# Half-row matmuls in sections of three feature groups, and eight PSUM banks dealt out anew, in a scan and gated-MLP kernel

## The chip, the cores and the metric

The kernel runs on one core of one Trainium2 chip. The metric is the device time of one execution, in microseconds (us), as the median of several runs. TensorE (PE) does the matmuls and writes to PSUM, which has eight banks of 2 KB in each of 128 partitions; ScalarE (ACT) and VectorE (DVE) read PSUM and do the element-wise work; GpSimd (POOL) does small constants; SyncE (SP) issues the DMAs. Each engine works through its own list of instructions, and semaphores tie the lists together.

## The reference

The input `x` has 2048 tokens of 448 features. It is normalised per token, and the result feeds two branches:

```python
def _A_ref(x, ...):                       # a diagonal complex recurrence over the tokens
    Lam_bar = jnp.exp(dt * Lam)
    Bu = jnp.einsum("bld,pd->blp", x + 0j, B_bar)
    for t in range(L):
        h = Lam_bar[None, :] * h + Bu[:, t, :]
        hs.append(h)
    return 2.0 * jnp.einsum("blp,dp->bld", hseq, Cmat).real + x * Dskip

def _B_ref(x, w_gate, w_up, w_down):      # a gated MLP, 448 -> 1792 -> 448
    h = _sigmoid(x @ w_gate) * (x @ w_up)
    return h @ w_down

xn = _layernorm(x)
return x + _A_ref(xn, ...) * _silu(_B_ref(xn, ...))
```

All data is bf16; the recurrence has 448 complex states.

## The kernel before

**Chunks.** The tokens are worked in four chunks of 512 (`NCH`, `TC`), and each chunk in four token tiles of 128. Features lie on the partitions: `xnT[c]` holds the normalised chunk, transposed. The 448 features are three full tiles of 128 rows and one half tile of 64.

**Gate and up.** The 1792 hidden features are 14 groups of 128 (`ft`). For a group, the gate matmuls add up in one PSUM bank and the up matmuls in another: three "wholes" each, over 128 rows (`gu_wholes`, L618), and one "half" each, over the last 64 rows (`gu_halves`, L611). The gate's half uses rows 0 to 63 of the array and the up's half rows 64 to 127, so the two run as a pair, side by side. In `emit_gu`, an even group runs its wholes and then its halves, an odd group its halves and then its wholes; so the halves of two groups stand together, and TensorE goes from 128-row to 64-row work and back once for two groups. Such a stretch of halves is called a section here. `gu_out` then has ScalarE take the sigmoid of the gate (`sig`, L635) and copy the up (`ub`, L639), and VectorE multiply the two (`hF`, L644); the multiplication of one group is put into the list when the next group's `gu_out` is written.

**Recurrence.** For a chunk and a tile `pt` of the states, `bu_halves` (L469) and `emit_bu` (L480) form the input of the recurrence, real and imaginary in one bank each (the last tile, of 64 states, has both in one bank). Its halves stand in the section of an odd group. ScalarE copies the banks (`bus`, L489, L549), and VectorE's pieces follow: `p0` to `p2`, two scans, `p3` to `p5` for the full tiles (L495 to L530), `q0` to `q7` for the last one (L555 to L591). For the last tile the two halves of the partitions are exchanged by a pair of DMAs, once before `q1` (`bsw`) and once before `q5` (`wsw`, L460, L461). The result is the state tile `h`.

**Down, y and the end.** `emit_down` (L660) multiplies a token tile of the finished chunk's `hF` by `w_down` into a bank `d`; ScalarE reads it twice (`sigd`, `zb`), and VectorE forms the gate `g_t`. `emit_y` (L682 to L688) sums the states' outputs into a bank `y`, and `emit_fin` (L695, L697) multiplies by the gate, adds `x` and stores. Down products of a chunk stand between the groups of the next chunk, y behind them.

**Order.** `keep_order` fixes every engine's list as the program writes it. VectorE's pieces wait in the list `pieces`; each call of `fill(pe, own)` moves a clock on by one and a budget `room` by what TensorE's work beside it is taken to last, and puts pieces into the list while there is room and the wait that a piece names (in ticks since the one before) is over. Extra work (statistics of the next chunk's x, the constants, `emit_c` with `c_tmp`, the transposes `tc_re` and `tc_im`, loads) is hung on a group with `at(c, ft, ...)` and written behind that group.

**Banks.** The PSUM pool has the tags `g` and `u` with two banks each and `acc` with four; `acc` serves `bu`, `d` and `y`, and in the opening the transposes `tp_x` and the gate and up of the third and fourth group. Banks of a tag are used in turn, and a tile waits until the one that held its bank before has been read.

**Opening.** The first four groups of chunk 0 run in two column halves of 256, as soon as the first two token tiles are normalised.

Of the kernel before, what the change touches and what calls it, by code (L numbers as in the profile page):

```python
# [10 lines left out]
FP32 = mybir.dt.float32  # L11
BF16 = mybir.dt.bfloat16
# [51 lines left out]
def kernel(  # L64
# [122 lines left out]
    warm_ps = ps.tile([P, P], FP32, name="warm_ps", tag="u")  # L187
# [74 lines left out]
    def ln_out(j, tp, copy):  # L262
        copy(out=xnT[0][:, :, j * P:(j + 1) * P], in_=tp[:])  # L263
# [28 lines left out]
    def emit_vecs():  # L292
        tp = ps.tile([P, KT, 4], BF16, name="tp_v", tag="g")
        turn_twice(tp, rows, 4)
        vec = w.tile([P, KT, 4], FP32, name="vec")
        dve.tensor_copy(out=vec[:], in_=tp[:])
        dt_b = w.tile([P, KT], BF16, name="dt_b")
        act.activation(dt_b[:], vec[:, :, 0], ACT.Exp)
        K.update(dt=dt_b, lim=vec[:, :, 1], lre=vec[:, :, 2], dsk=vec[:, :, 3])
# [154 lines left out]
    def bank(spare, tag, name):  # L454
        if spare:
            return ps.tile([P, TC], FP32, name=name, tag="acc", bufs=4)
        return ps.tile([P, TC], FP32, name=name, tag=tag)
# [16 lines left out]
    def emit_bu(c, pt, pst):  # L474
# [71 lines left out]
        else:  # L546
# [47 lines left out]
            for cost, f, wait in ((0.42, q0, 1), (0.42, q1, 1), (0.42, q2, 0), (1.27, q3, 0), (0.42, q4, 0),  # L594
                                  (0.42, q5, 2), (0.0, q6, 0), (0.42, q7, 0)):
                later(cost, f, wait)
# [23 lines left out]

    def emit_gu(c, ft, beside_halves=None):
        gt, ut = bank(False, "g", "g_ps"), bank(False, "u", "u_ps")
        if ft % 2 == 0:
            gu_wholes(c, ft, gt, ut, True, up_first=(c == 0 and ft == 4))
            gu_halves(c, ft, gt, ut, False)
        else:
            gu_halves(c, ft, gt, ut, True)
            if beside_halves is not None:
                beside_halves()
            gu_wholes(c, ft, gt, ut, False)  # L630
        gu_out(c, ft, gt, fp.tile([P, TC], BF16, name="ub"), ut)
# [25 lines left out]
    def emit_down(c, j):  # L657
        d = ps.tile([P, D], FP32, name="d_ps", tag="acc", bufs=4)
# [18 lines left out]
    def emit_y(c, j, d0=0, d1=D):  # L677
        y = ps.tile([P, D], FP32, name="y_ps", tag="acc", bufs=4)
# [69 lines left out]
    tps = [ps.tile([P, KT + 1, P], BF16, name="tp_x", tag="acc", bufs=4) for _ in range(TPC)]  # L748

    def norm0(j):  # L750
        ln_norm(0, j)
        ln_turn(0, j)
# [7 lines left out]
    act.activation(K["r"][:], K["arg"][:], ACT.Exp)  # L760
    ln_root(0, 2, 2, True)
    ln_out(0, tps[0], dve.tensor_copy)
# [6 lines left out]
    gus = [(bank(ft > 1, "g", "g_ps"), bank(ft > 1, "u", "u_ps")) for ft in range(4)]  # L769
# [8 lines left out]
    ln_out(3, tps[3], dve.tensor_copy)  # L778
    for ft in range(4):
        gu_halves(0, ft, *gus[ft], ft == 3, 0, HC)  # L780
    gu_wholes(0, 3, *gus[3], False, 0, HC)
    gu_wholes(0, 3, *gus[3], True, HC, TC)
    for ft in (3, 0, 1, 2):
        gu_halves(0, ft, *gus[ft], ft < 3, HC, TC)
    for ft in range(3):
        gu_wholes(0, ft, *gus[ft], False, HC, TC)
# [45 lines left out]
    bu_q, out_q, bu_pst = [], [], []  # L832
    room[0] = -2.0
    for c in range(NCH):
        bu_q.extend((c, pt) for pt in range(KT))
        for ft in range(4 if c == 0 else 0, FT):
            bu = None
            if ft % 2 == 1 and (4 if c == 0 else 0) < ft < FT - 1 and bu_q and unread[0] < 2:
                bu = bu_q.pop(0)
                emit_gu(c, ft, lambda: bu_pst.append(bu_halves(*bu)))  # L840
            else:
                emit_gu(c, ft)
            emit_gate()
            for cost, f in beside.pop((c, ft), ()):
                room[0] -= cost
                f()
            fill(1.62 if c < NCH - 1 or ft < 9 else 2.2, 0.42)
            if ft % 2 == 0:
                continue
            if bu is not None:  # L850
                emit_bu(*bu, bu_pst.pop())
                popped[0] = clock[0]
                fill(1.5, 0.0)
            if c == 0:
                continue
            if ft < 8:
                emit_down(c - 1, ft // 2)
                fill(2.66, 0.39)
                if ft == 7:
                    out_q.extend((c - 1, j) for j in range(TPC))  # L860
            if c == NCH - 1 and ft == FT - 1:
                emit_mul()
            for _ in range(2 if ft == 11 else 1):
                if not (out_q and ft >= 8 and all((out_q[0][0], pt) in hs for pt in range(KT))):
                    break
                emit_y(*out_q[0])
                emit_fin(*out_q.pop(0))
                fill(1.53, 1.01)
    flush()

# [6 lines left out]
    def outs(j, d0=0, d1=D):  # L877
        emit_y(c, j, d0, d1)
        emit_fin(c, j, d0, d1)

    for j in range(2):
        down(j)
        outs(j)
    down(2)
    down(3)
    outs(2)
# [33 lines left out]
```

## Time and profile before

| | |
|---|---|
| three runs | 193.56, 193.94 and 194.0 us; median 193.94 |
| the profiled execution | 193.69 us, of which the span from first to last instruction is 191.9 us |
| TensorE busy | 186.2 us (97%), 1080 matmuls, granted clock 1.00 |
| VectorE busy | 156.4 us (81%) |
| ScalarE busy | 111.1 us (58%) |
| GpSimd busy | 49.3 us (26%) |
| DMA | 14.87 MB in all, mean 77 GB/s |

In the lines of a timeline the columns are: start in us from the span's start, length in us, engine, line of the program, operation, output <- inputs, shapes, how many instructions are merged, and in brackets the idle time before them with what ended it. A line of the waits reads: who waited, for whom, us in total, how often, the longest. Matmuls overlap, so the time from start to start, not the length, is what one costs. L numbers are lines of the kernel before; in the changed kernel the same statements stand some ten lines higher (L623 and L627 for `sig` and `ub`, L632 for `hF`, L648 for d, L670 and L672 for y, L683 for `sg`).

### The profile page before, as it was taken

The numbers are of one execution on the slowest core, as the hardware profiler recorded it, in microseconds if no ns is written. First come the engines' busy times: TensorE is split into PE (matmuls) and PEld (weight loads), VectorE is DVE, ScalarE is ACT, GpSimd is POOL, SyncE is SP. The second block draws the span as 40 slices with busy tenths as digits, with TensorE's granted clock in tenths as the row PEclk, the third lists the DMA queues.
The fourth block names the chain that finished last, engine by engine and source line by source line (L and its number), as shares of the span: only waits on it lengthen the run. The fifth ranks groups of instructions, "written<-read, shape, count | busy, mean of one in ns | idle before, by whom it ended". The sixth has DMA issues, their size and how long they took to land.

```text
span 191.9 us, 3117 instructions
## 1 busy us (share of the span) xinstructions
PE 186.2 (97%) x1080; PEld 89.1 (46%) x1080; DVE 156.4 (81%) x315; ACT 111.1 (58%) x213; POOL 49.3 (26%) x98
## 2 busy tenths in 40 slices
PE   7899999999999999999999999999999999999992
PEld 6765433344444445444444444444444444545552
DVE  3889799937999699999985979997649999995224
ACT  4997776557499775454556586245746744242240
POOL 3885399940043025030321020304020000000000
PEclk9999999999999999999999999999999999999999
DMA  5998993994410123601001000530010010021101
GB/s 145 310 301 160 254 112 70 321 286 105 90 31 0 36 87 88 97 26 29 0 5 27 0 0 24 108 89 16 0 27 3 0 27 0 26 65 38 44 6 48
DMA packets 27592, 14.87 MB, mean 77 GB/s; under 512 B 16308, under 2 KB 27576, under 8 KB 27576
## 3 DMA queue, kind: packets, MB, share of 16 engines
q1 hardware_dynamic: 27568, 14.67, 32.7%
q8 instruction: 8, 0.13, 0.3%
q14 instruction: 8, 0.07, 0.2%
q10 hardware_dynamic: 8, 0.00, 0.0%
HBM read 8.38 MB, written 1.84 MB: 53 GB/s over the span
## 4 chain that ended last, share of the span: by engine, by line
PE 91%; DMA 4%; DVE 2%; SPq 1%; issue 0%
PE d_ps L660 22%; PE g_ps L618 20%; PE u_ps L618 18%; PE bu L480 9%; PE y_ps L682 9%; PE g_ps L611 7%; DMA b_re<-in_A_B_re_dram 2%; PE bu L469 2%; PE y_ps L688 2%; PE y_ps L684 1%; DMA x<-in_A_x_dram 1%; DVE sg L695 1%; DVE frac L398 1%; DVE xn L243 0%; DVE o_t L697 0%
## 5 line engine op out<-in xcount | busy, mean ns | idle before, releaser
L635 ACT ACTIVATE sig<-g_ps 128x512 bf16<-128x512 f32 x56 | 33.1, 597 | 36.8 <-PE u_ps L611 32.4
L618 PE MATMUL g_ps<-xnT,wg 128*128 128x512 bf16 (+1 forms) x180 | 46.4, 366 | 0.2 <-DVE xnT L263 0.2
L618 PE MATMUL u_ps<-xnT,wu 128*128 128x512 bf16 (+1 forms) x180 | 45.9, 365 | 0.0
L660 PE MATMUL d_ps<-wd,hF 128*128 128x448 bf16 x224 | 44.8, 352 | 0.0
L639 ACT CAST ub<-u_ps 128x512 bf16<-128x512 f32 x52 | 30.3, 583 | 2.1 <-PE u_ps L618 0.4
L660 PEld LDWEIGHTS <-hF 128*128 128x128 bf16 x224 | 21.7, 98 | 20.5
L663 ACT ACTIVATE sigd<-d_ps 128x448 bf16<-128x448 f32 x16 | 8.7, 543 | 32.4 <-PE d_ps L660 30.4
L618 PEld LDWEIGHTS <-wu 128*128 128x128 bf16 x180 | 17.6, 98 | 18.5
L644 DVE TENSOR_TENSOR hF<-sig,ub 128x512 bf16<-128x512 bf16 x56 | 23.5, 423 | 2.2 <-ACT ub L639 2.1
L618 PEld LDWEIGHTS <-wg 128*128 128x128 bf16 x180 | 14.7, 98 | 22.0 <-issue 12.0
L508 DVE TENSOR_TENSOR_SCAN wv<-r_col,st,ta 128x512 bf16<-128x512 f32 x18 | 22.7, 1273 | 0.2
L682 PE MATMUL y_ps<-ct,h 128*128 128x448 bf16 (+1 forms) x102 | 21.0, 342 | 0.0
L480 PE MATMUL bu<-xnT,bT 128*128 128x512 bf16 x84 | 20.7, 379 | 0.0
L515 POOL TENSOR_TENSOR tq<-wv,smT 128x2 f32<-128x2 bf16 x9 | 5.3, 585 | 56.2 <-DVE wv L508 56.2
L611 PE MATMUL u_ps<-xnT,wt 64*128 64x512 bf16 (+1 forms) x60 | 17.0, 367 | 0.1
L611 PE MATMUL g_ps<-xnT,wt 64*128 64x512 bf16 (+1 forms) x60 | 17.0, 367 | 0.0
L669 DVE TENSOR_TENSOR g_t<-zb,sigd 128x448 bf16<-128x448 bf16 x16 | 6.2, 390 | 11.9 <-ACT zb L665 11.9
L489 ACT CAST bus<-bu 128x512 bf16<-128x512 f32 x24 | 13.6, 592 | 0.5
L207 DVE BATCH_NORM_STATS2 stats<-x 128x6 f32<-128x448 bf16 x14 | 8.6, 617 | 6.2 <-DMA x<-in_A_x_dram 6.2
L682 PEld LDWEIGHTS <-h 128*128 128x128 bf16 x102 | 9.6, 98 | 8.2
L480 PEld LDWEIGHTS <-bT 128*128 128x128 bf16 x84 | 8.2, 98 | 9.9
L695 DVE TENSOR_TENSOR sg<-y_ps,g_t 128x448 bf16<-128x448 f32 (+1 forms) x17 | 10.0, 588 | 0.9 <-PE y_ps L688 0.5
(135 smaller groups left out, 225.3 us busy)
## 6 DMA issues: line engine op xcount, KB each, us to landing
out_dram<-o_t SPq DMA_DIRECT2D x15, 112.0 KB, 1.8
wd<-in_B_w_down_dram SPq DMA_DIRECT2D x1, 1568.0 KB, 7.7
x<-in_A_x_dram SPq DMA_DIRECT2D x3, 448.0 KB, 3.6
wg<-in_B_w_gate_dram SPq DMA_DIRECT2D x2, 384.0 KB, 5.2
wu<-in_B_w_up_dram SPq DMA_DIRECT2D x2, 384.0 KB
wg<-in_B_w_gate_dram SPq DMA_DIRECT2D x1, 576.0 KB, 4.4
wu<-in_B_w_up_dram SPq DMA_DIRECT2D x1, 576.0 KB, 6.5
bsw<-bus SPq DMA_DIRECT2D x8, 64.0 KB, 2.0
```

Of the source, the lines that this page charges most:

```text
L480: pe.matmul(pst[:], lhsT=bT[:, kt, lo:hi], rhs=xnT[c][:, kt, :], start=False, stop=(kt == 2))
L489: act.copy(out=bus[:, cc, :], in_=pst[cc][:])
L508: dve.tensor_tensor_scan(out=T["wv"][:, cc, :], data0=rb, data1=T["ta"][:, cc, :], initial=(0.0 if c == 0 else st[pt][:, cc, :]), op0=mul, ...
L611: pe.matmul(t[:, n0:n1], lhsT=wt[p0:p0 + 64, f0:f1], rhs=xnT[c][p0:p0 + 64, KT if c == 0 and p0 else 3, n0:n1], start=first, stop=not first)
L618: pe.matmul(t[:, n0:n1], lhsT=wm[:, kt, f0:f1], rhs=xnT[c][:, kt, n0:n1], start=(first and kt == 0), stop=(not first and kt == 2))
L635: act.activation(sig[:], gt[:], ACT.Sigmoid)
L639: act.copy(out=ub[:], in_=ut[:])
L644: dve.tensor_tensor(out=h[:], in0=sig[:], in1=ub[:], op=ALU.mult)
L660: pe.matmul(d[:], lhsT=hF[c, ft][:, j * P:(j + 1) * P], rhs=wd[:, ft, :], start=(ft == 0), stop=(ft == FT - 1))
L663: act.activation(sigd[:], d[:], ACT.Sigmoid)
L682: pe.matmul(y[:, d0:d1], lhsT=hs[c, pt][:, cc, sl], rhs=ct[:, 2 * pt + cc, d0:d1], start=(pt == 0 and cc == 0), stop=False)
L695: dve.tensor_tensor(out=sg[:, d0:d1], in0=ys[c, j][:, d0:d1], in1=gs[c, j][:, d0:d1], op=ALU.mult)
```

## The change

- Banks: `g` and `u` get three banks each, `acc` two.
- Groups are worked in sections of three, at a chunk's end of two: chunk 0 in groups 4-6, 7-9, 10-11, 12-13; the others in 0-2, 3-5, 6-8, 9-11, 12-13. In a section, all groups but the last run their wholes, then all halves stand together, with those of a bu, then the last group runs its wholes.
- Extra work that hangs on a group is written behind that group's wholes for all but the last of a section (before its `gu_out`), and behind the `gu_out` of the last.
- Per chunk there are five sections (four in chunk 0) and so five chances for a bu; a bu is taken while fewer than three are unread (before: two). Chunk 0 takes four. Chunks 1 and 2 take theirs in their sections 0, 1, 3 and 4, chunk 3 in 0 to 3.
- Down products stand one each behind sections 0 and 1 and two behind section 2; y in pairs behind sections 3 and 4. In the end, d(3,1) stands ahead of y(3,0), and y uses the banks of `u`.
- The waits of `q1` and `q5`, in ticks, go from 1 and 2 to 2 and 3.
- In the opening, the fourth group starts with its wholes, and its halves of the first columns stand in the second section; the transposes' tiles are made when they are needed.

```diff
-    warm_ps = ps.tile([P, P], FP32, name="warm_ps", tag="u")
+    warm_ps = ps.tile([P, P], FP32, name="warm_ps", tag="u", bufs=3)
...
     def bank(spare, tag, name):
         if spare:
-            return ps.tile([P, TC], FP32, name=name, tag="acc", bufs=4)
-        return ps.tile([P, TC], FP32, name=name, tag=tag)
+            return ps.tile([P, TC], FP32, name=name, tag="acc", bufs=2)
+        return ps.tile([P, TC], FP32, name=name, tag=tag, bufs=3)
...
-            for cost, f, wait in ((0.42, q0, 1), (0.42, q1, 1), (0.42, q2, 0), (1.27, q3, 0), (0.42, q4, 0),
-                                  (0.42, q5, 2), (0.0, q6, 0), (0.42, q7, 0)):
+            for cost, f, wait in ((0.42, q0, 1), (0.42, q1, 2), (0.42, q2, 0), (1.27, q3, 0), (0.42, q4, 0),
+                                  (0.42, q5, 3), (0.0, q6, 0), (0.42, q7, 0)):
...
-    def emit_gu(c, ft, beside_halves=None):
...
-    def emit_y(c, j, d0=0, d1=D):
-        y = ps.tile([P, D], FP32, name="y_ps", tag="acc", bufs=4)
+    def emit_y(c, j, d0=0, d1=D, tag="acc", bufs=2):
+        y = ps.tile([P, D], FP32, name="y_ps", tag=tag, bufs=bufs)
...
-    tps = [ps.tile([P, KT + 1, P], BF16, name="tp_x", tag="acc", bufs=4) for _ in range(TPC)]
+    tps = []
     def norm0(j):
+        tps.append(ps.tile([P, KT + 1, P], BF16, name="tp_x", tag="acc", bufs=2))
...
-    gus = [(bank(ft > 1, "g", "g_ps"), bank(ft > 1, "u", "u_ps")) for ft in range(4)]
+    gus = [(bank(False, "g", "g_ps"), bank(False, "u", "u_ps")) for _ in range(3)]
...
+    gus.append((bank(True, "g", "g_ps"), bank(True, "u", "u_ps")))
+    for ft in range(3):
+        gu_halves(0, ft, *gus[ft], False, 0, HC)
+    gu_wholes(0, 3, *gus[3], True, 0, HC)
+    gu_halves(0, 3, *gus[3], False, 0, HC)
     for ft in range(4):
-        gu_halves(0, ft, *gus[ft], ft == 3, 0, HC)
-    gu_wholes(0, 3, *gus[3], False, 0, HC)
-    gu_wholes(0, 3, *gus[3], True, HC, TC)
-    for ft in (3, 0, 1, 2):
-        gu_halves(0, ft, *gus[ft], ft < 3, HC, TC)
-    for ft in range(3):
+        gu_halves(0, ft, *gus[ft], True, HC, TC)
+    for ft in range(4):
         gu_wholes(0, ft, *gus[ft], False, HC, TC)
...
+    def rest(c, ft):
+        emit_gate()
+        for cost, f in beside.pop((c, ft), ()):
+            room[0] -= cost
+            f()
+
+    def section(c, units, bu):
+        gb, more = {}, 0.6 if c == NCH - 1 and units[0] >= 9 else 0.0
+        pre, post = units[:-1], units[-1]
+        for ft in pre:
+            gb[ft] = (bank(False, "g", "g_ps"), bank(False, "u", "u_ps"))
+            gu_wholes(c, ft, *gb[ft], True, up_first=(c == 0 and ft == 4))
+            rest(c, ft)
+            fill(1.3 + more, 0.0)
+        for ft in pre:
+            gu_halves(c, ft, *gb[ft], False)
+        gb[post] = (bank(False, "g", "g_ps"), bank(False, "u", "u_ps"))
+        gu_halves(c, post, *gb[post], True)
+        pst = None if bu is None else bu_halves(*bu)
+
+        def out(ft):
+            gu_out(c, ft, gb[ft][0], fp.tile([P, TC], BF16, name="ub"), gb[ft][1])
+
+        out(pre[0])
+        fill(0.2 + 0.22 * len(units), 0.42)
+        if bu is not None:
+            emit_bu(*bu, pst)
+            popped[0] = clock[0]
+            fill(1.5, 0.0)
+        if len(pre) > 1:
+            out(pre[1])
+            room[0] -= 0.42
+        gu_wholes(c, post, *gb[post], False)
+        out(post)
+        rest(c, post)
+        fill(1.3 + more, 0.42)
...
+        cuts = (4, 7, 10, 12, 14) if c == 0 else (0, 3, 6, 9, 12, 14)
+        for si in range(len(cuts) - 1):
+            section(c, range(cuts[si], cuts[si + 1]), bu_q.pop(0) if bu_q and unread[0] < 3 else None)
+            last = c == NCH - 1 and si == len(cuts) - 2
+            if last:
+                emit_mul()
+            for _ in range(2 if si == 2 else 1):
+                if d_q:
+                    emit_down(*d_q[0])
+                    out_q.append(d_q.pop(0))
+                    fill(2.66, 0.39)
+            for _ in range(2 if si > 2 else 0):
+                if out_q and all((out_q[0][0], pt) in hs for pt in range(KT)):
+                    emit_gate()
+                    emit_y(*out_q[0])
+                    emit_fin(*out_q.pop(0))
+                    fill(1.53, 1.01)
...
-    for j in range(2):
-        down(j)
-        outs(j)
-    down(2)
-    down(3)
-    outs(2)
+    down(0)
+    for j in range(3):
+        down(j + 1)
+        outs(j)
     outs(3, 0, D // 2)
     outs(3, D // 2, D)
```

## The prediction

> **What bounds the kernel now.** The page's first part, then the chain that ended last:
>
> ```profile
> PE 186.2 (97%) x1080; PEld 89.1 (46%) x1080; DVE 156.4 (81%) x315; ACT 111.1 (58%) x213; POOL 49.3 (26%) x98
> PE 91%; DMA 4%; DVE 2%; SPq 1%; issue 0%
> ```
>
> From 15.9 us on, TensorE runs without a gap; the kernel is TensorE's list of matmuls. So I price what leaves that list (TensorE's timeline), then look for the first product that now comes too late for it (the orders of the changed kernel on each engine, laid against the rows of before). A switch, TensorE's timeline:
>
> ```profile
> 30.78 0.81 PE L618 MATMUL u_ps<-xnT,wu 128*128 128x512 bf16 x3
> 31.53 0.39 PE L611 MATMUL g_ps<-xnT,wt 64*128 64x512 bf16 x1
> 31.53 0.39 PE L611 MATMUL u_ps<-xnT,wt 64*128 64x512 bf16 x1
> 31.75 0.38 PE L611 MATMUL g_ps<-xnT,wt 64*128 64x512 bf16 x1
> 31.76 0.38 PE L611 MATMUL u_ps<-xnT,wt 64*128 64x512 bf16 x1
> 32.06 0.82 PE L618 MATMUL g_ps<-xnT,wg 128*128 128x512 bf16 x3
> 32.72 0.59 PE L618 MATMUL u_ps<-xnT,wu 128*128 128x512 bf16 x2
> ```
>
> From wholes to halves to wholes: a whole takes 0.216 ((32.72-32.06)/3, less the switch), as does a pair of halves. The last up whole starts at 31.21 (30.78+2x0.216), the first gate whole behind the halves at 32.06: 0.85 where three pitches make 0.65; with the 0.01 by which the second whole is late, a section of halves costs 0.215 for its two switches, however many pairs stand in it.
>
> SyncE's queue and ScalarE around 50 us:
>
> ```profile
> 41.39 5.11 SPq L167 DMA_TRANSPOSE tc_re<-c_re  x4
> 46.60 5.12 SPq L167 DMA_TRANSPOSE tc_im<-c_im  x4
> 51.82 0.54 SPq L460 DMA_DIRECT2D bsw<-bus  x1
> 52.40 0.59 SPq L461 DMA_DIRECT2D bsw<-bus  x1
> ```
> ```profile
> 52.55 0.60 ACT L635 ACTIVATE sig<-g_ps 128x512 bf16<-128x512 f32 x1 [0.65 <-PE u_ps L611]
> 53.05 0.58 ACT L639 CAST ub<-u_ps 128x512 bf16<-128x512 f32 x1
> 53.52 0.68 ACT L437 ACTIVATE c_tmp<-tc_im,nci 128x448 f32<-128x448 bf16 x1
> 54.09 0.67 ACT L437 ACTIVATE c_tmp<-tc_re,nci 128x448 f32<-128x448 bf16 x1
> 54.65 0.59 ACT L635 ACTIVATE sig<-g_ps 128x512 bf16<-128x512 f32 x1
> ```
>
> The last tc_im transpose starts at 50.46 and lands 2.4 later (the DMA rows), at 52.9; the first c_tmp, which reads it, starts at 53.52, only 0.6 behind. The tail, VectorE's timeline and a row of the waits:
>
> ```profile
> 169.61 1.28 DVE L567 TENSOR_TENSOR_SCAN wv<-r_col,st,ta 128x512 bf16<-128x512 f32 x1
> ...
> 174.40 0.42 DVE L578 TENSOR_TENSOR td<-wsw,spm 128x512 bf16<-128x512 bf16 x1 [1.42 <-DMA wsw<-wv]
> 174.86 0.42 DVE L591 TENSOR_TENSOR h<-tcs,td 128x512 bf16<-128x512 bf16 x1
> ```
> ```profile
> PEld L684 <- DVE h L591: 0.2, 1, 0.2
> ```
>
> VectorE works from 143.2 to 173.0 without a stop, and the first y of chunk 3 still waits 0.2 for its last state tile, h3. There is no slack at the end.
>
> **The change, part by part** (us; against the profiled execution: span 191.9, time 193.69, 0.25 under the median of the runs, 193.94).
>
> *Sections.* Before: 5 in chunk 0 and 7 in each other chunk, 26; after: 4 and 5, 19. Seven fewer by 0.215: **-1.51**. Matmuls stay 1080.
>
> *Opening.* Before, the fourth group's first halves wait for the copies of xnT (11.37 and 11.77), with 12 wholes, a section of four pairs and 18 wholes behind: the 512-wide work starts at 15.90. After, its up wholes wait for the same copy until 11.77 and end at 12.10; a section of five pairs (0.74) and 24 wholes at 0.109 follow: 15.46. **-0.43**. The normalised tiles now share two banks, and the third waits for the first's copy (ends 8.15) before 10.2: nothing, 2 us of cover.
>
> *ScalarE behind the transposes, chunk 1.* Two moves meet. The swap pair of bu(0,3) is now issued in chunk 0, and stands in SyncE's queue between tc_re and tc_im. And a group's extra work runs behind its wholes: the first two c_tmp stand ahead of the gate-and-up of groups 3 to 5 and of the two `bus` copies of bu(1,1), no longer behind a group's sigmoid. tc_re starts about 41.25 (its load of c ends it, as before); 5.21 for four, 1.18 for the swap pair, 3.86 to the last tc_im, 2.4 to land: 53.9. ScalarE then does 0.57+0.56 (c_tmp), 0.50+0.47 (sig, ub), 0.59 (bus): 56.65. That copy frees the bank for the down product behind group 5, as bu and d rotate through two banks. TensorE is there at 15.46 + 60 wholes and 10 pairs of chunk 0 (15.10) + bu 5.39 (three of a pair and six wholes, 1.51; the fourth half of that) + 4 sections 0.86, and for chunk 1: 36 wholes and 6 pairs (9.06), two bu 3.02, two sections 0.43, one d 2.65: 51.97. **+4.7**. Bounds: without the swap pair's 1.18 it is 3.5; with one of the pauses that SyncE's queue shows (a transpose of 2.63 instead of 1.27) 6.0. I take the rows as they stand. Statistics of x, which VectorE awaits until 44.10 in before, hold the first d's last weights by some 0.3; absorbed here.
>
> *The tail.* In chunk 2 the last bu moves from group 11 to the section of 12 and 13, and its pieces wait for more ticks (`q1` 2, `q5` 3). Let T be the start of the d behind groups 3 to 5 of chunk 3. The second bu copy of that section starts at T-1.07 (its last matmul starts 1.51 ahead of T and ends 0.38 later), sig and ub of group 4 follow, ending at T+0.46; VectorE's product of group 4 waits for them with `q1` behind it. Then 0.34 (hF), 0.46+0.46 (`q1`, `q2`), 1.31 (scan), 2.65 (swap: issue 138.07, reader 140.68), 0.82 (td, h3): T+6.5. Only then does chunk 3's list begin: three bu blocks of 6.36 (143.18 to 149.87 less an hF of 0.33), 8 hF of 0.335, 2 g_t of 0.31, 4 pairs sg and o_t of 0.96, bu 3 to its scan 2.57: 28.8, and some 0.4 in wait for a late ub; then swap 2.65, td and h3 0.9: **T+39.2**. TensorE from T: five d 13.25, groups 6 to 13 12.1 (48 wholes, 8 pairs) and 3 sections 0.65, two bu 2.37, four y 6.06, then the seventh matmul of y(3,0) 1.13: **T+35.5**. +0.1 to load: **+3.8**, less the 0.2 of before. Part of it may show a d earlier, where the first d of chunk 3 awaits the bank that sg(2,2) frees; the end is the same. Bounds: 2.5 (VectorE 0.4 without idle time, and its list 0.8 or 3% shorter) to 4.7 (the last swap of before took 3.49).
>
> *Other banks and the end.* A d elsewhere follows its bu copies by about 1.1 (the second ends at T-0.48, the first 0.6 sooner). y in u's banks, d(3,1) ahead of y(3,0): the list behind d(3,3) is unchanged, nothing; cover is d's 2.65 against sigd and zb's 1.0.
>
> Sum: -1.51 -0.43 +4.7 +3.8 -0.2 = +6.4, so **200.0** (193.69 + 6.4 = 200.1, rounded down as the waits can only partly fail).
>
> **Rivals.**
>
> *The clock falls in the gap* (201.9). Warm-up matmuls, TensorE's timeline:
>
> ```profile
> 1.35 2.96 PE L191 MATMUL warm_ps<-ident 128*128 128x128 bf16 x26 [1.35 <-POOL ident L125]
> 7.28 0.78 PE L191 MATMUL warm_ps<-ident 128*128 128x128 bf16 x11
> ```
>
> After idling, 0.107 apiece (2.69/25); later 0.056 (0.56/10). Between them a batch of 18 runs from 4.57 in 1.42, 4 gaps at the slow and 13 at the fast rate, so the full rate comes some 3.7 after the first matmul. If a gap of 4.7 sets TensorE back, 3.7 at half rate cost +1.9. No gap over 1.35 stands in before, so the price lies between 0 and 1.9; I take 0, by the 0.61 gap at 6.6, behind which the rate stays full. The Trainium skill (TensorE: Matmul & The Clock Gate, What's actually happening) has the clock fall after an idle window of some 3.4 us that runs freely; by it, an estimate, a gap of 4.7 meets one in about 4 of 10 cases, and the sum would be 201.9 in those. No run here shows it. Chance 0.25.
>
> *Banks starve everywhere* (203). If copies came over 1.1 later than laid out, all ten bu-then-d places would wait, 0.3 each: +3. ScalarE at 58% speaks against. The Trainium skill (Perfetto Trace Analysis, Matmuls) asks that independent groups rotate through different banks so that evacuation overlaps; two for bu, d and y is the least that does, and the 1.1 says it holds here. Chance 0.05.
>
> *The transposes are in time* (195.3): tc_im landed by 49.2, so no ACT wait; -2.1 + 3.8. The loads of c would have to end 4.7 sooner. Chance 0.07. *VectorE is in time* (196.2): only the ScalarE wait. Chance 0.08.
>
> *TensorE's list alone decides* (191.8, faster): both products arrive ahead of it, and only -1.94 is left. It decides from T+35.5 for h3 and 49.2 for tc_im; for it speaks that VectorE has 19% idle time in all, against it that the 30 us before 173 have none. Chance 0.04.
>
> **How the numbers follow.** The forecast as laid out has 0.5, the last hundredth goes to no change. Range 196.0 to 202.2: below it lie the transposes in time, the list alone and no change (0.12), above it starved banks (0.05); the forecast's own bounds give 197.6 (193.69-2.14+3.5+2.5) to 202.2 (193.69-2.14+6.0+4.7). A measurement here tells 0.3% from no change: faster 0.04, same 0.02, slower 0.94.
>
> **What would show it.** 19 sections; the 512-wide work from about 15.5. TensorE idle some 4 to 5 ahead of a d near 52, ended by ScalarE's bus, with ScalarE idle ahead of c_tmp until 53 to 54, put down to the DMA of tc_im. At the end, TensorE idle 3 to 4.5 in all, ended by VectorE's h3 and sg. Wrong if ScalarE's c_tmp starts before 50, if VectorE reaches the scan of chunk 3's h3 while TensorE still is at chunk 2's y, or if matmuls behind the gap stand 0.43 apart.

## The result

The changed kernel takes 203.31 us (median of four runs, 201.04 to 204.9) against 193.86 of the kernel before, measured beside it: a ratio of 1.0451, with a 95% interval of 1.0359 to 1.0543. Two later measurements gave 204.66 and 203.69 (ratios 1.0545 and 1.0539). It is slower by 4.5 to 5.5%, where 200.0 was forecast with a range of 196.0 to 202.2. The profiled run of after took 202.79, with a span of 200.7. Ratios leave out runs that count as disturbed by a low clock; since the clock is part of what is studied here, single times and medians are given over all runs.

The page of after, its first part, TensorE's row and clock row of the second part (40 slices of 5.0 us each), and the engines of the chain that ended last:

```profile
PE 187.9 (94%) x1080; PEld 90.9 (45%) x1080; DVE 156.8 (78%) x315; ACT 109.4 (54%) x213; POOL 45.0 (22%) x98
...
PE   7899999999489999999999999999999999985993
...
PEclk9999999999969999999999999999999999999699
...
PE 59%; DMA 14%; DVE 13%; SPq 8%; issue 2%; ACT 1%; POOL 1%; ACTq 0%; DVEq 0%
```

TensorE was 91% of the chain before and is 59% now. Its row has two holes, at the eleventh slice and near the end, and one slice behind each hole the granted clock reads 6 in place of 9: something happens there that is not a wait.

The waits of TensorE (releaser, total us, times, longest):

```profile
PE d_ps L648 <- ACT bus L489: 3.6, 1, 3.6
PE y_ps L672 <- DVE h L591: 2.0, 1, 2.0
...
PE d_ps L648 <- DVE sg L683: 1.1, 1, 1.1
...
PE u_ps L618 <- DMA wu<-in_B_w_up_dram: 0.3, 1, 0.3
```

The first hole, in the timelines of SyncE's queue, ScalarE and TensorE of after (start, duration, and in brackets the idle time ahead of the instruction with its releaser):

```profile
40.51 5.11 SPq L167 DMA_TRANSPOSE tc_re<-c_re  x4
45.67 0.59 SPq L460 DMA_DIRECT2D bsw<-bus  x1
46.30 0.59 SPq L461 DMA_DIRECT2D bsw<-bus  x1
46.94 5.18 SPq L167 DMA_TRANSPOSE tc_im<-c_im  x4
```
```profile
53.45 0.67 ACT L437 ACTIVATE c_tmp<-tc_im,nci 128x448 f32<-128x448 bf16 x1 [6.09 <-DMA tc_im<-c_im]
54.03 0.65 ACT L437 ACTIVATE c_tmp<-tc_re,nci 128x448 f32<-128x448 bf16 x1
54.59 0.57 ACT L623 ACTIVATE sig<-g_ps 128x512 bf16<-128x512 f32 x1
55.06 0.57 ACT L627 CAST ub<-u_ps 128x512 bf16<-128x512 f32 x1
55.53 1.08 ACT L489 CAST bus<-bu 128x512 bf16<-128x512 f32 x2
```
```profile
51.80 0.81 PE L618 MATMUL u_ps<-xnT,wu 128*128 128x512 bf16 x3
56.17 4.21 PE L648 MATMUL d_ps<-wd,hF 128*128 128x448 bf16 x14 [3.56 <-ACT bus L489]
60.21 0.81 PE L618 MATMUL g_ps<-xnT,wg 128*128 128x512 bf16 x3
...
181.77 1.30 PE L670 MATMUL y_ps<-ct,h 128*128 128x448 bf16 x6
185.10 0.37 PE L672 MATMUL y_ps<-ct,h 128*128 128x448 bf16 x1 [2.03 <-DVE h L591]
185.30 0.54 PE L676 MATMUL y_ps<-diag,xnT 128*128 128x128 bf16 x4
185.65 4.33 PE L648 MATMUL d_ps<-wd,hF 128*128 128x448 bf16 x14
189.82 1.30 PE L670 MATMUL y_ps<-ct,h 128*128 128x448 bf16 x6
```

This is the queue order and the ScalarE order that the prediction laid out, with the wait of c_tmp ended by the DMA of tc_im at 53.45. By start times TensorE loses 3.72 (the three up wholes end their turn at 51.80 + 0.65 = 52.45). Then the 14 matmuls of d take 4.04 to the next start (56.17 to 60.21), where 14 at 0.189 make 2.65; for most of that time they stand 0.373 apart. The d near the end takes 4.17. So behind each hole some 1.4 to 1.7 are lost without any wait. The granted clock says why. Stretches of 3.41 us around the two holes (length, then busy time and count of PE, PEld, DVE, ACT and POOL; the last three columns are the mean granted clock, the DMA share and GB/s):

```profile
52.21:55.63 3.42, 0.40 (x2) 0.10 (x1) 1.48 (x3) 2.18 (x5) 0.00 (x0) 1.00 0.15 30
55.63:59.04 3.41, 2.87 (x8) 1.13 (x8) 2.19 (x6) 3.41 (x9) 0.00 (x0) 0.50 0.02 5
...
181.92:185.33 3.41, 1.38 (x9) 0.53 (x7) 1.20 (x5) 0.97 (x2) 0.00 (x0) 1.00 0.16 38
185.33:188.75 3.42, 3.42 (x14) 1.65 (x13) 1.33 (x4) 0.00 (x0) 0.00 (x0) 0.50 0.10 34
```

The clock is at one half for exactly one stretch of 3.41 us behind each hole. The two begin 129.70 apart, which is 38 times 3.413: they sit on one fixed grid.

The account of the profiled run, to the end of TensorE's list (188.18 before, 196.95 after, +8.77): sections -1.51, opening -0.43, a wait for the up weights of groups 8 and 9 +0.46, first hole +3.72, half rate behind it +1.39, d and y(3,0) in the tail +1.2 and +2.2 by start times, half rate behind them +1.7, the 0.2 of before's own wait gone; together +8.5, so 0.2 is left over. The rest of the 9.1 between the two profiled runs (193.69 to 202.79) lies behind TensorE's list.

### The profile page after: what moved, and what is told of

Same layout as the page of the kernel before. It is cut to its first block, busy times and chain, and to the rows that moved or that the text cites. A ratio compares the mean times of both kernels' runs of the same rounds, so it can differ in the third digit from the quotient of the medians.

```text
span 200.7 us, 3098 instructions
## 1 busy us (share of the span) xinstructions
PE 187.9 (94%) x1080; PEld 90.9 (45%) x1080; DVE 156.8 (78%) x315; ACT 109.4 (54%) x213; POOL 45.0 (22%) x98
## 4 chain that ended last, share of the span: by engine, by line
PE 59%; DMA 14%; DVE 13%; SPq 8%; issue 2%; ACT 1%; POOL 1%; ACTq 0%; DVEq 0%
PE d_ps L648 19%; PE g_ps L618 11%; PE u_ps L618 11%; PE bu L480 6%; PE y_ps L670 6%; SPq L167 4%; PE g_ps L611 4%; DMA x<-in_A_x_dram 4%; DMA c_re<-in_A_C_im_dram 4%; DMA b_re<-in_A_B_re_dram 3%; SPq L252 2%; DVE sg L683 2%; DVE hF L632 1%; DVE wv L508 1%; DMA tc_im<-c_im 1%
## 5 line engine op out<-in xcount | busy, mean ns | idle before, releaser
L623 ACT ACTIVATE sig<-g_ps 128x512 bf16<-128x512 f32 x56 | 33.7, 607 | 37.4 <-PE u_ps L611 31.6
L648 PE MATMUL d_ps<-wd,hF 128*128 128x448 bf16 x224 | 47.2, 368 | 4.6 <-ACT bus L489 3.6
L618 PE MATMUL g_ps<-xnT,wg 128*128 128x512 bf16 (+1 forms) x180 | 45.9, 365 | 0.3 <-DVE xnT L263 0.2
L648 PEld LDWEIGHTS <-hF 128*128 128x128 bf16 x224 | 22.6, 102 | 27.4 <-issue 8.5
L627 ACT CAST ub<-u_ps 128x512 bf16<-128x512 f32 x52 | 30.9, 595 | 0.5
L618 PEld LDWEIGHTS <-wg 128*128 128x128 bf16 x180 | 16.9, 98 | 18.3 <-issue 2.0
L515 POOL TENSOR_TENSOR tq<-wv,smT 128x2 f32<-128x2 bf16 x9 | 3.1, 347 | 64.5 <-DVE wv L508 64.5
L611 PE MATMUL g_ps<-xnT,wt 64*128 64x512 bf16 (+1 forms) x60 | 15.7, 365 | 0.0
L611 PE MATMUL u_ps<-xnT,wt 64*128 64x512 bf16 (+1 forms) x60 | 15.7, 365 | 0.0
L480 PEld LDWEIGHTS <-bT 128*128 128x128 bf16 x84 | 6.9, 98 | 12.9 <-issue 6.8
```

The costliest lines, as they stand in the source:

```text
L480: pe.matmul(pst[:], lhsT=bT[:, kt, lo:hi], rhs=xnT[c][:, kt, :], start=False, stop=(kt == 2))
L611: pe.matmul(t[:, n0:n1], lhsT=wt[p0:p0 + 64, f0:f1], rhs=xnT[c][p0:p0 + 64, KT if c == 0 and p0 else 3, n0:n1], start=first, stop=not first)
L618: pe.matmul(t[:, n0:n1], lhsT=wm[:, kt, f0:f1], rhs=xnT[c][:, kt, n0:n1], start=(first and kt == 0), stop=(not first and kt == 2))
L623: act.activation(sig[:], gt[:], ACT.Sigmoid)
L627: act.copy(out=ub[:], in_=ut[:])
L648: pe.matmul(d[:], lhsT=hF[c, ft][:, j * P:(j + 1) * P], rhs=wd[:, ft, :], start=(ft == 0), stop=(ft == FT - 1))
```

## The experiments

Each edit is against the changed kernel, unless it says otherwise. The experiments ran on different chips; times are compared with the kernel before as measured beside them (193.62 to 193.85).

**c_tmp two groups later.** Takes the ScalarE steps that wait for tc_im out of the way of the bu copy.

```diff
-        at(1, 4 + i // 2, 0.68, lambda i=i: emit_c(i))
+        at(1, 6 + i // 2, 0.68, lambda i=i: emit_c(i))
```

> The changed kernel, with the seven c_tmp steps (ScalarE's products with the transposed c) planned two groups later in chunk 1, behind groups 6 to 9 instead of 4 to 7; nothing else. My theory: the first gap (3.7 us of TensorE at 52.2) is ScalarE standing in its order before c_tmp, which waits for the tc_im transpose, with the bu copy behind it. Without c_tmp ahead of that copy the gap goes (-3.7) and the half-rate stretch behind it goes with it (-1.4). The tail stays late, since chunk 2's pieces of VectorE still have the longer counts; 1 to 3.4 us of it are left, with or without its own half-rate stretch (1.7). So 195 to 198.5 us. Rival, that the banks starve by themselves (two banks for bu, d and y are too few wherever a bu and a d meet): the gap stays at 2 us or more with a ScalarE copy as its releaser, and the time stays above 200.

194.47 (194.43 to 195.11), ratio 1.005 [1.0036, 1.0064]. The waits of this kernel:

```profile
PE y_ps L672 <- DVE h L591: 0.8, 1, 0.8
...
PE d_ps L648 <- DVE sg L683: 0.5, 1, 0.5
PE d_ps L648 <- DVE hF L632: 0.4, 1, 0.4
```

The row of ScalarE's bus is gone, and with it the half rate. The place of these steps made 8.6 of the 9.4 us: the tail's waits fell to 1.3 as well. c_tmp's cost counts in the budget by which VectorE's pieces are given out, and in the trace the order of VectorE's list differs from 54 to 173 us. That side effect was larger than expected (the time is 0.5 below the forecast's low end). No matmul waits for a ScalarE copy of bu any more; the 0.5 for sg is still a wait for a bank, since this d takes the bank of an earlier y, and it comes from VectorE being late.

**q5's count alone.**

```diff
-                                  (0.42, q5, 3), (0.0, q6, 0), (0.42, q7, 0)):
+                                  (0.42, q5, 2), (0.0, q6, 0), (0.42, q7, 0)):
```

> The changed kernel, with the count of ticks that piece q5 of a bu chain waits for set from 3 back to 2; nothing else. If the long count of q5 is what makes VectorE late in the tail, the tail's two waits (1.2 and 2.2) and the half-rate stretch behind them go: 198 us. My theory, that the place of the last bu of chunk 2 (section of groups 12 and 13 instead of 11) is the larger part, leaves 2 us or more of the tail: 201.5 to 203.5 us, no more than 1.5 better than the changed kernel. The first gap stays at 3.7 by both.

203.66 (202.2 to 203.77), ratio 1.0499 [1.047, 1.0529]: no gain. Both tail waits stand as in after (0.99 and 2.03), as does the first hole (4.24 here). q5 by itself is not the tail's cause.

**Both edits.**

> Both edits together: c_tmp two groups later and q5's count 2. If each wait of TensorE that the change brought comes from the order on ScalarE and VectorE, and none from the sections or the banks themselves, no wait over 0.5 us is left but that for the weights of groups 8 and 9 at 23.5 (0.46), the clock stays full, and the time is TensorE's list: 193.69 less 1.51 and 0.43 plus 0.46, 192.2; range 191.9 to 193.5. So it would be faster than the kernel before by 0.9%. Rival, that two banks for bu, d and y starve: waits of 0.3 at each of ten places, 195 or more.

192.81 (192.38 to 193.18), ratio 0.9958 [0.9945, 0.9971]: 0.4% faster than the kernel before, with the interval clear of 1. Clock 1.0, no wait over 0.2 behind 21 us. It misses 192.2 by 0.6, and the timeline shows where:

```profile
18.62 0.38 PE L611 MATMUL g_ps<-xnT,wt 64*128 64x512 bf16 x1
18.92 0.37 PE L611 MATMUL u_ps<-xnT,wt 64*128 64x512 bf16 x1
18.93 0.39 PE L469 MATMUL bu<-xnT,bT 64*128 64x512 bf16 x1
19.86 0.37 PE L469 MATMUL bu<-xnT,bT 64*128 64x512 bf16 x1 [0.54 <-DVE ub L789]
```

A half of group 6 and one of bu wait for VectorE's copies of u, which stand behind two statistics of x that waited 1.15 for their load. The bu's wholes start at 20.16 where 19.13 was due (its start in after), 1.02 lost; the bracket shows only 0.54, since the two delayed halves also break their pairing.

**tc_im ahead of the swap pair.** Both groups of transposes issued at group 12 of chunk 0.

```diff
-        at(0, 12 + i, 0.0, lambda nm=nm: [emit_c_turn(nm, kt) for kt in range(KT)])
+        at(0, 12, 0.0, lambda nm=nm: [emit_c_turn(nm, kt) for kt in range(KT)])
```

> The changed kernel, with both groups of c transposes issued at group 12 of chunk 0, so that tc_im stands ahead of the swap pair of bu(0,3) in SyncE's queue; nothing else. My theory has two parts of the first gap: 1.2 from the swap pair ahead of tc_im in the queue, the rest (2.5) from c_tmp's place ahead of the copy on ScalarE. So the gap shrinks from 3.7 to 2.5 and the time by 1.2, to 201.6 if the half-rate stretch behind the gap stays, to 200.2 if it goes. If the queue were the whole cause, the gap would go altogether: 198.

201.29 (200.88 to 201.58), ratio 1.0391 [1.0375, 1.0407]. SyncE's queue and the d behind the hole:

```profile
45.54 5.12 SPq L167 DMA_TRANSPOSE tc_im<-c_im  x4
50.76 0.55 SPq L460 DMA_DIRECT2D bsw<-bus  x1
```
```profile
54.62 4.49 PE L648 MATMUL d_ps<-wd,hF 128*128 128x448 bf16 x14 [2.27 <-ACT bus L489]
```

tc_im starts 0.1 behind tc_re's end, and the hole is 2.27 in place of 3.56. The swap pair's share is 1.3, where 1.2 was worked out; the larger share is c_tmp's place on ScalarE. The half-rate stretch behind the hole stayed in the profiled run (mean clock 0.98); the other three runs have 0.989 to 0.991, about one stretch fewer, without being clearly faster.

**Idle matmuls ahead of the bu.** The first of four runs that ask whether idling makes the slow stretches.

```diff
+        if c == 1 and post == 5:
+            for _ in range(12):
+                pe.matmul(gb[post][0][:], lhsT=wg[:, 0, 0:P], rhs=xnT[c][:, 0, :], start=True, stop=True)
         gu_halves(c, post, *gb[post], True)
```

> The changed kernel, with 12 matmuls of 128x512 added to TensorE's list in chunk 1, into the gate bank of group 5 ahead of its halves, which overwrite them: 2.6 us of idle work (12 x 0.216) that lies inside the first gap; the output is unchanged. My theory: the d product behind the gap ran at 0.373 instead of 0.189 a matmul for 3.41 us because TensorE had idled there and its granted clock fell to half. With the gap cut from 3.7 to 1.1 the clock stays full, the d goes at 0.189, and the time falls by 1.4 in spite of the added work: 201.9 us (201.0 to 202.6). If the slow matmuls come from the data (weights of wd or hF late) and not from idling, the d stays slow and the time stays within 0.5 of the changed kernel or goes up.

205.09 (204.58 to 206.25), ratio 1.0596 [1.0564, 1.0627]: the forecast of 201.9 failed. c_tmp began at 56.85, 3.4 later than in after: tc_re started 1.86 later (42.37), and the last transpose of tc_im took 1.55 longer to land (4.14 against 2.59 from its start to c_tmp). So the hole moved along with the added work and stayed 3.23 long. What the run does show is a hole of 3.23 with no half rate behind it. Stretches of this run, laid on the grid of its later fall at 187.89:

```profile
54.78:58.19 3.41, 1.57 (x8) 0.59 (x6) 0.63 (x2) 1.34 (x3) 0.00 (x0) 1.00 0.02 2
58.19:61.60 3.41, 2.02 (x11) 1.07 (x11) 3.04 (x8) 3.41 (x8) 0.00 (x0) 1.00 0.00 0
184.48:187.89 3.41, 1.38 (x12) 0.61 (x10) 1.64 (x5) 0.47 (x2) 0.00 (x0) 1.00 0.16 38
187.89:191.30 3.41, 3.41 (x11) 1.41 (x10) 0.83 (x2) 0.00 (x0) 0.00 (x0) 0.50 0.10 34
```

The long hole was cut by a border of the grid, with 1.57 and 2.02 of TensorE's work left in the two stretches, and the clock stayed; the shorter hole near the end lay inside one stretch, left 1.38, and the clock fell. So it is not the length of a hole that decides, but how busy TensorE is in one stretch of the grid.

**A section in every group** (against the kernel before).

```diff
-            gu_halves(c, ft, gt, ut, True)
+            gu_wholes(c, ft, gt, ut, True)
+            gu_halves(c, ft, gt, ut, False)
             if beside_halves is not None:
                 beside_halves()
-            gu_wholes(c, ft, gt, ut, False)
```

> The kernel before, with a section of halves in every group instead of one for two groups: 52 sections in place of 26, the same 1080 matmuls. It measures the price of a section by itself. By the working of the prediction, 0.215 for each: +5.6, 199.3 us. By the rows behind the change (0.095 into the halves, 0.09 out of them, 0.19 together): +4.9, 198.6. If the switch were hidden beside the weight loads, 193.7.

199.11 (199.04 to 199.17), ratio 1.0279 [1.0265, 1.0293]: +5.49 for 26 more sections, with no wait of TensorE in it, so 0.211 for a section.

**The counts as before** (q1 1, q5 2).

```diff
-            for cost, f, wait in ((0.42, q0, 1), (0.42, q1, 2), (0.42, q2, 0), (1.27, q3, 0), (0.42, q4, 0),
-                                  (0.42, q5, 3), (0.0, q6, 0), (0.42, q7, 0)):
+            for cost, f, wait in ((0.42, q0, 1), (0.42, q1, 1), (0.42, q2, 0), (1.27, q3, 0), (0.42, q4, 0),
+                                  (0.42, q5, 2), (0.0, q6, 0), (0.42, q7, 0)):
```

> The changed kernel, with the counts of ticks of the bu chain's pieces as they were before (q1 1, q5 2); the sections, banks, the place of chunk 2's last bu and of c_tmp stay. My theory of the tail: the counts hold 2 of its 3.2 us of waits, the later place of the last bu the rest; the wait of y(3,0) for h3 goes, a d waits about 1.3, and without a gap near 2 us the second half-rate stretch (1.7) does not come: 199.5 us (198.8 to 200.5). If the place of the bu were the whole cause, both waits stay and the time with them, 202.5 to 204.

200.78 (200.3 to 201.97), ratio 1.0386 [1.0355, 1.0417], within its range. In the profile the wait for h3 (2.03) is gone and no half rate follows in the tail; a d still waits 1.13 for sg. So the counts hold about 2 of the tail, and q1's is needed for it, since q5's alone changed nothing. What holds the other 1.1 is not shown: the run with both edits has chunk 2's last bu in the same place and no wait in the tail, so that place is not enough by itself, and c_tmp's cost in the budget has a part in it. The first hole was 4.27 in this run. The other three runs have a mean clock of 0.982 to 0.983 against 0.989 in the profiled one, so about one stretch more at half rate; where it lay is not known.

**Copies of u ahead of the statistics** (on top of both edits).

```diff
-    ln_stats(TPC)
     gu_out(0, 0, gus[0][0], ubs[0])
     gu_out(0, 1, gus[1][0], ubs[1])
-    ln_stats(TPC + 1)
     gu_out(0, 2, gus[2][0], ubs[2], up_copy)
     gu_out(0, 3, gus[3][0], ubs[3], up_copy)
+    ln_stats(TPC)
+    ln_stats(TPC + 1)
```

> The kernel with c_tmp two groups later and q5's count 2, and beside that the two statistics of chunk 1's first x tiles moved on VectorE behind the copies of u of groups 2 and 3. In the run without this edit those statistics waited 1.15 for the load of x, with the copies behind them, and TensorE lost 1.02 at 18.6 (a half and a bu half that waited for these copies' banks). If that is what kept it 0.6 above 192.2, the time is 191.8 (191.5 to 192.3); if the later statistics cost a first d 0.3 us, 192.1; if the opening's wait comes from elsewhere, 192.8 as before.

192.34 (192.27 to 192.75), ratio 0.9933 [0.992, 0.9946]. The wait of the bu is gone; the wait for the up weights of groups 8 and 9 is now in sight (0.25 in the bracket, 0.46 by start times), which is what separates it from 191.8.

**The changed kernel again, and late idle matmuls.** In the second the 12 matmuls stand behind the bu, and group 5's halves behind them:

```diff
-        gu_halves(c, post, *gb[post], True)
+        late = c == 1 and post == 5
+        if not late:
+            gu_halves(c, post, *gb[post], True)
...
+        if late:
+            for _ in range(12):
+                pe.matmul(gb[post][0][:], lhsT=wg[:, 0, 0:P], rhs=xnT[c][:, 0, :], start=True, stop=True)
+            gu_halves(c, post, *gb[post], True)
         gu_wholes(c, post, *gb[post], False)
```

> The changed kernel itself once more, as the comparison for the next run on the same chip, and for its own spread. Each stretch at half rate lasts 3.41 us and costs 1.4 to 1.7; the waits make the same 7.2 us in every run. So the single times should lie in steps of about 1.5 to 2 by the number of such stretches, as the mean granted clock counts them: about 201 with one, 203 with two, 205 with three. If the spread comes from transfers instead, time and clock go apart.

204.66 (202.96 to 205.5). The steps are only partly there. At nearly the same mean clock (0.981 to 0.983) times go from 202.96 to 205.03; the first hole was 4.34 here against 3.56 in the first profile, since tc_re began at 42.28 in place of 40.51. So the clock alone does not make the spread; in the profiles of the changed kernel and of the runs with its c_tmp in place, tc_re begins anywhere between 40.33 and 42.37, which moves the hole. In this run two stretches in a row were at half rate (55.84 to 62.66), the first with 1.31 of work in it.

> The changed kernel, with the idle work put into the gap itself: in chunk 1, behind the bu of group 5's section, 12 matmuls of 128x512 into group 5's gate bank (2.6 us), and then the group's halves, which overwrite them (a section of their own, 0.2); the output is unchanged. In the run with these matmuls ahead of the bu the gap did not shrink, because the transposes ended later in that run, and nothing was settled. Here nothing that ScalarE waits for stands behind the added work, so the gap shrinks from about 3.9 to about 1.1, and TensorE ends the d no later. If idling is what lowers the clock, the first half-rate stretch goes and the time falls by 1.4 (1.0 to 1.7) against the changed kernel of the same call; if the d's slow pace comes from its data, the time is the same within 0.5.

204.42 over six runs, 202.11 to 206.09: no gain that can be told from the 204.66. The last transpose landed late again (3.34 from its start to c_tmp) and left a hole of 2.28. The single runs go with the clock: 202.11 at 1.0, 203.4 and 203.59 at 0.99, 205.25 to 206.09 at 0.98. The profiled one is that at 1.0. Both its holes were cut by the grid, laid here from its only fall, behind the last matmul:

```profile
54.58:58.00 3.42, 1.45 (x8) 0.58 (x7) 1.71 (x3) 2.41 (x5) 0.00 (x0) 1.00 0.01 0
58.00:61.41 3.41, 3.10 (x17) 1.58 (x17) 2.08 (x7) 3.41 (x8) 0.00 (x0) 1.00 0.00 0
184.29:187.70 3.41, 1.60 (x12) 0.97 (x13) 2.43 (x6) 0.00 (x0) 0.00 (x0) 1.00 0.08 19
```

**Banks and opening alone** (the kernel before with three banks each for gate and up and two for the rest, and the changed opening, but its own loop).

> The kernel before, with the changed kernel's banks (three each for gate and up, two for bu, d, y and the opening's tiles) and its opening, but its own loop over pairs of groups, with sections, counts and extra work as they were. The rival of the banks: with two banks for bu, d and y an order that was laid out for four has each d and y wait for the copies of the tile two before. By its order laid against the rows of before, the first bu would wait 1.2, the d of chunk 1 behind group 11 2.0, two y 0.8 and 1.0, another d 0.7 and some 0.2 in four places: +6.2, 200. If two banks are enough in any order, only the opening's gain is left: 193.2. My forecast is 199 (197 to 201); it would show that the changed loop is what makes two banks enough.

200.19 (200.01 to 201.21), ratio 1.0345 [1.0324, 1.0365], with the clock at 1.0. Two rows of its waits:

```profile
PE d_ps L660 <- ACT bus L489: 2.4, 2, 1.8
PE y_ps L682 <- ACT bus L489: 1.4, 2, 0.8
```

With 1.1 of the first bu that is 4.9, in the places laid out. By start times, matmul for matmul against the kernel before, the losses are larger than the brackets: 1.48 at the first bu, 1.96 and 0.73 at two d, 0.74 and 1.01 at two y, 0.2 at each of five more d and 0.1 at the end, 7.0 in all; less 0.43 of the opening that is the measured +6.5. Two banks for bu, d and y do starve in the old order; in the changed loop, once c_tmp is out of the way, none of these rows is there. The banks need the loop.

**The weights earlier** (on top of the copies' edit).

```diff
-        if pt == 1:
+        if pt == 0:
             load_w(sync, 1024, F)
```

> The kernel with c_tmp two groups later, q5's count 2 and the copies of u ahead of the statistics (192.34), and beside that the last load of the gate and up weights issued one step of the loop over bT earlier (about 2.5 us). Its profile has one wait left, that of the up wholes of groups 8 and 9 for these weights (0.46 from the gap in the rows). With the weights in time: 191.9 (191.6 to 192.3); if the earlier load only pushes the transposes of B late, 192.3 or more with a bu that waits for bT.

191.84 (191.71 to 192.46), ratio 0.991 [0.9897, 0.9923]: 0.9% faster than the kernel before, with the interval clear of 1. TensorE's row and clock row of this kernel:

```profile
PE   7999999999999999999999999999999999999992
...
PEclk9999999999999999999999999999999999999999
```

This is the change's worth on TensorE's list alone: 193.69 less 1.48 (seven sections at 0.211) and 0.43 is 191.8.

**Filling the holes.** The same edit with 16 for 12; then also 9 idle matmuls in a free gate bank ahead of y(3,0); both with the changed kernel on the same chip. The second adds:

```diff
+    idle = bank(False, "g", "g_ps")
     for j in range(3):
         down(j + 1)
+        if j == 0:
+            for _ in range(9):
+                pe.matmul(idle[:], lhsT=wg[:, 0, 0:P], rhs=xnT[c][:, 0, :], start=True, stop=True)
         outs(j)
```

> The changed kernel once more, as the comparison on the same chip: 203 to 205 us, mean granted clock 0.97 to 0.99.

203.69 (203.35 to 206.09), ratio 1.0539 [1.05, 1.0578], clock 0.972 to 0.983.

> As the run with late idle matmuls, with 16 in place of 12 (3.45 us, and 0.2 for the halves' own section), so that at most 0.7 of the first gap is left; the output is unchanged. In the run with 12 a gap of 2.3 was left, and its runs fell on both sides. If the slow d comes from idling alone, no stretch at half rate follows in any run, the d behind it goes at 0.189, and the median lies 1.4 (1.0 to 2.0) below the changed kernel of the same call, with 3.65 us more work on TensorE. If it comes from the d's data or from what else runs then, no change within 0.5.

202.4 (202.11 to 203.65), ratio 1.0461 [1.0436, 1.0486], clock 0.989 to 1.0: 1.3 less than the changed kernel with 3.65 more work on TensorE; the time is as expected. The hole was 1.77, not at most 0.7, yet the stretch that holds it had 1.64 of work and the one behind it ran at full rate. In three of the six runs the clock is still 0.989 to 0.991, about one stretch at half rate; only the first hole was filled here, and which hole made it is not known.

> The same, and 9 idle matmuls (1.94 us) into a free gate bank ahead of y(3,0), in the gap where its seventh matmul waits 2.03 for h3; the output is unchanged. By my theory both falls of the clock go: mean granted clock 0.99 to 1.0 in every run, the d's at 0.189, and the time 3.1 (2.5 to 3.6) below the changed kernel of the same call, near 201, with single runs within 1 of each other but for the landing of the transposes; 5.6 us of idle work would make the kernel faster. If the clock is not the cause, it is as the changed kernel, or up to 0.5 slower.

202.25 (201.9 to 202.76), ratio 1.0439 [1.0425, 1.0452], clock 0.997 to 1.0 in all four runs, and the d products at 0.189:

```profile
58.77 2.81 PE L648 MATMUL d_ps<-wd,hF 128*128 128x448 bf16 x14 [1.66 <-ACT bus L489]
...
182.98 2.11 PE L908 MATMUL g_ps<-xnT,wg 128*128 128x512 bf16 x9
184.92 1.30 PE L670 MATMUL y_ps<-ct,h 128*128 128x448 bf16 x6
...
186.71 2.81 PE L648 MATMUL d_ps<-wd,hF 128*128 128x448 bf16 x14
```

So idling is the cause of the slow stretches: the same d on the same data goes at full rate once TensorE is kept busy, in all four runs, where no run of the changed kernel had a mean clock above 0.991. The gain is 1.4, not 3.1, mainly because the first d starts 2.07 later than in the profile of the changed kernel measured beside it (58.77 against 56.70). Of that, 1.17 is the start of tc_re (42.21 against 41.04) and 0.90 the last transpose of tc_im (3.49 against 2.59 from its start to c_tmp). In the profile with 16 idle matmuls alone c_tmp starts 4.4 behind the start of the last transpose (51.46 to 55.84), in the changed kernel's 2.6 (51.38 to 53.98). It was late in the first two filled runs too. Why the last transpose lands later in all four filled runs was not found.

## Why the prediction was too low

**Right: the places and their order.** Sections: 19 in place of 26; the price of 0.215 measured as 0.211. Opening: the 512-wide work starts at 15.47, worked out as 15.46. The first hole is ended by ScalarE's bus, behind c_tmp, behind tc_im; moving c_tmp removes it and moving tc_im shortens it by the swap pair's time. The tail waits for VectorE's sg and h3.

**Right with a size off: both waits.** The first was worked out as 4.7 and is 3.72: tc_re started at 40.51, not 41.25, and TensorE came 0.46 later on account of the weights. It was 4.3 in the profiles of both later runs of the changed kernel, so the term has a spread of its own, inside the bounds given (3.5 to 6.0). The tail was +3.8 and is 3.4, within 2.5 to 4.7; h3 of chunk 2 ends at T+6.6, worked out as T+6.5. Two slips in the working change nothing: the last bu of chunk 0 is counted in the 5.39 with 0.86, not with half of 1.51, and the terms up to 56.65 add up to 56.59.

**Missed: the weights of groups 8 and 9 (+0.46).** Before, group 8's up wholes began at 26.04; with sections of three they come ahead of the halves and the bu, at 23.67, and reach the load before it lands. The prediction followed VectorE's and ScalarE's products, and did not ask whether a matmul moved forward meets a load. The copies of u behind the statistics of x, which cost 1.0 in other runs, were not looked for either.

**Wrong: "I take 0" for the clock.** This is the step that failed. The prediction had the mechanism as a rival, priced for one hole, +1.9, with a chance of 0.25. It came in the first hole (+1.39) and again in the tail (+1.7), where the prediction did not consider it at all. Its own sign, matmuls behind the gap at half their rate, was there. The 0.61 gap in the warm-up, from which zero was taken, could not tell: the stretch of the clock's grid that holds it (5.12 to 8.54 of before) still had 2.66 us of work, and the clock falls only below some 1.4. With 3.1 for the two stretches and 0.46 for the weights, less 1.4 for the two waits, the working's 200.1 becomes 202.3 for the profiled run of 202.79. Of the 0.5 left, 0.3 lies behind TensorE's list; the median, 203.31, is another 0.5 up, within the spread of the runs.

The Trainium skill (TensorE: Matmul & The Clock Gate, What's actually happening) has the clock fall after an idle window of some 3.4 us that runs freely. The runs agree on the window and on its running freely: the half-rate stretches are 3.41 long and sit on one grid whose place differs from run to run. They differ on what counts as idle, as the next but one section shows with 1.38 us of work.

The rivals that the banks starve everywhere, that the transposes or VectorE are in time, and that the list alone decides are ruled out for the changed kernel; the last is what the repaired kernel reaches.

## What to carry to other kernels

When a plan takes time off the bound engine, look in each other engine's order for a step that now stands ahead of a copy which frees a bank, and at every matmul that was moved forward for the load it meets: here the place of one set of steps was worth 8.6 us and the gain itself 1.8 (193.66 to 191.84). A hole in TensorE's work is not paid by its length alone; add 1.4 to 1.7 us for each one that may leave TensorE less than some 1.4 us of work in a stretch of 3.4, and do so for each hole. A plan that counts ticks and budgets ties stages together: a cost moved in chunk 1 changed the waits behind chunk 3.

## What the hardware showed beside that

TensorE's granted clock was decided in stretches of 3.413 us. In the profiles of these runs the clock was at one half in the stretch that followed one with 0 (twice), 0.11, 0.40, 1.14, 1.18, 1.31 or 1.37 to 1.38 us of TensorE work (the last in six profiles), and stayed full after 1.45, 1.57, 1.60, 1.64, 1.75 and 2.02. Where the list ends, it fell after 1.40 (q5 alone) and 1.41 (c_tmp later) and not after 1.56 and 1.65 (both in profiles of the changed kernel). Laid on the grid from the first rise of the clock on, no stretch of the 17 profiles departs from this. So the border lies between 1.41 and 1.45 of 3.41, about 42% busy: a gap of 2.03 us is enough if it falls whole into one stretch, while one of 3.23 us that is cut by a border costs nothing more. For 1.14, the stretch and its follower, in the run with tc_im ahead:

```profile
51.54:54.95 3.41, 1.14 (x6) 0.48 (x5) 2.32 (x6) 3.05 (x7) 0.00 (x0) 1.00 0.16 38
54.96:58.37 3.41, 3.41 (x11) 1.36 (x9) 2.11 (x5) 3.17 (x7) 0.00 (x0) 0.50 0.02 5
```

Where the grid lies changes from run to run, so a kernel with such holes has a spread that a kernel without them lacks: 201.04 to 206.09 over all runs of the changed kernel, 193.54 to 194.21 for the one before. With both holes filled, four runs lay within 0.9 of each other.
